# One attention block on one Trainium2 core: every engine's whole program and the list of loads as fixed lists

## The chip, the cores and the metric

The kernel runs on one core of a Trainium2 chip. The time is the device time of one execution in microseconds (us). The engines named here are TensorE (PE; its weight loads are shown as PEld), VectorE (DVE), ScalarE (ACT) and SyncE (SP, whose queue issues all loads and stores). GpSimd (POOL) only writes the identity matrix at the start. Each engine works off its own program in order, and the engines wait for one another through semaphores.

## What is computed

```python
B, Sq, D = 8, 112, 640
H, Sk, Dh = 32, 512, 192
q = (x @ wq).reshape(B, Sq, H, Dh)              # transposed to b h q d
scores = einsum("bhqd,bhkd->bhqk", q, k_cache) * Dh ** -0.5
p = softmax(scores, axis=-1)
o = einsum("bhqk,bhkd->bhqd", p, v_cache)       # transposed to b q (h d)
return o @ wo
```

All arrays are bfloat16. The caches have 8 x 32 x 512 x 192 elements each, wq is 640 x 6144 and wo 6144 x 640.

## The kernel before

**Steps.** The 32 heads are taken in two halves of 16. A unit t (0 to 15) is one batch element and one half of the heads. A step n (0 to 63) is a quarter of a unit, four heads, so unit t has the steps 4t to 4t+3. Two neighbouring units (two batch elements) share one product with wq and one with wo: m numbers these pairs (0 to 7) and lp the pairs of heads in them (0 to 7).

**Operations.** The program is a set of named operations, each with its engine, its dependencies and its instructions (class Plan, line 12). On TensorE they are:

- ("X", c) transposes a block of x (line 281), and ("K", t, u) a head of k for the first two units (line 295). From unit 2 on k arrives transposed, through a transposing load (line 149) on SP's queue.
- ("Qa", m, lp) and ("Qb", m, lp) are the two parts of q = x wq for two heads, 10 and 5 matmuls (line 329).
- ("S", n) is the scores of a step: 16 whole matmuls and then 16 on half of the rows each (lines 384 to 399). They always use the banks 0 to 3 of PSUM (of 8).
- ("PT", n, j) transposes the softmax of two heads (line 447), and ("PV", n) multiplies it with v (lines 475 and 486).
- ("O", u, f, part) is a piece of o wo (line 520), in 14 groups u of four pieces f, of 12 or 24 matmuls, cut in two parts. ("O6", ...), ("OL", ...) and ("OF", b) are the last group in other cuts and the final transposes of the output (lines 559, 583 and 608).

Each of these leaves its result in a bank, and the next user of the bank waits until it has been taken out. ScalarE takes out q (evQa, evQb, line 335), the values (evPV, line 496) and half of the transposed softmax (evPT with j = 0, line 453), and computes the exponentials with their sums (exp, line 417). VectorE takes out the scores with their minimum into one of two buffers (smax, line 412), divides (rc, norm, lines 429 and 421), takes out the other half of the transposed softmax (evPT with j = 1), adds up the output (oacc, lines 536 and 538), and makes the copies of q (qc, lines 361 and 362): two copies that put parts of q from partitions 0 to 63 into 64 to 127 and the other way round, since a head has 192 = 128 + 64 rows. Results of "X" and "K" go to either of the two. S(n+1) waits for the four smax of step n and for qc(n+1); smax(n, i) waits for the exp two before it; PV(n) waits for both evPT(n).

**The order.** Three stretches set it. The first nine steps follow lists written out by hand, FRONT_PE, FRONT_ACT and FRONT_DVE (lines 711 to 770), and the loads follow FRONT_SP. The steps 9 to 57 come from a loop (lines 783 to 824): each step puts on TensorE S(n), PV(n-2), Qa, the first part of an O, PT(n-1), the rest of the O and Qb, and on the other engines a fixed pattern. Which q and which O fall into which step is told by q_at and o_at (lines 619 to 628): one q to a step, except in steps 18 and 19, which have none (q_at leaves them out), and one O. The last six steps follow TAIL and two lists (lines 265 to 274 and 838 to 859). In the steps 57 to 61 a transposing transfer on SP's queue, ("TD", n), does the work of PT.

**SP's queue.** Loads are issued in one order. ("KN", t, lo, n) loads k for the transposes on TensorE, ("K", t, 0) is the transposing load of a unit, ("V", t, 0 or 8) half a unit's v, ("WQ", half, lp) a piece of wq, ("WO", half, u) one half of a half's wo. V waits for the PV that last used its buffer, K(t) for the last S of unit t-2, and the second half's WQ and WO for the last use of the first half's.

## Time and profile before

| what | us |
|---|---|
| median of 3 runs | 453.37 (451.6 to 454.62) |
| the profiled execution | 452.17 |
| its span, first to last instruction | 450.2 |
| TensorE busy in the span | 438.4 (97%) |
| VectorE busy | 367.8 (82%) |
| ScalarE busy | 338.4 (75%) |

The granted clock of TensorE was 0.999. The profiled execution is 1.2 us under the median, and 1.97 us of it lie outside its span. A row of the timeline has the start, the time, the engine, the line and operation, the tiles and how many instructions are merged in it; in brackets stands the idle time ahead of it and what ended it. The time of a matmul in such a row includes its way through the array, so that neighbouring rows overlap: what one costs is read from its start to the start of the next.

### The profile page before, as it was taken

Reading aid. Unit: us, or ns where it says so; the run is one execution under the profiler, and the core shown is the slowest. Engines: PE = TensorE matmul, PEld = TensorE weight load, DVE = VectorE, ACT = ScalarE, POOL = GpSimd, SP = SyncE. Lnnn points to the kernel's source line nnn. Section 1 sums busy time; section 2 is a strip of 40 time slices with the busy share of each in tenths; the row PEclk is TensorE's granted clock in tenths of the full one; section 3 lists DMA queues with packets and bytes.
Section 4 is the critical chain, followed back from the end, with each engine's and each line's share of the span. In section 5 each row is a group of like instructions: output and inputs, shape, how many; then the busy total and the mean of one; then the engine's idle time right before and its main releaser. Section 6 shows DMA issues by size and latency. Waiting matters only on the chain.

```text
span 450.2 us, 15025 instructions
## 1 busy us (share of the span) xinstructions
PE 438.4 (97%) x6345; PEld 402.8 (89%) x6345; DVE 367.8 (82%) x1172; ACT 338.4 (75%) x787; POOL 0.7 (0%) x6
## 2 busy tenths in 40 slices
...
GB/s 296 373 376 359 238 302 245 250 328 277 261 275 279 315 240 352 232 336 258 274 290 232 287 229 341 261 261 363 227 306 187 276 220 217 273 244 269 223 193 67
DMA packets 232547, 121.94 MB, mean 271 GB/s; under 512 B 182560, under 2 KB 232480, under 8 KB 232480
## 3 DMA queue, kind: packets, MB, share of 16 engines
...
HBM read 73.50 MB, written 1.15 MB: 166 GB/s over the span
## 4 chain that ended last, share of the span: by engine, by line
PE 85%; DMA 6%; DVE 4%; ACT 4%; issue 1%; SPq 0%; DVEq 0%; ACTq 0%
PE ps L329 18%; PE ps L520 17%; PE ps L486 11%; PE ps L447 10%; PE ps L397 7%; PE ps L475 6%; PE ps L384 6%; PE ps L386 6%; DMA wo_sb<-in_wo_dram 3%; DVE s_sb L412 3%; ACT p_sb L417 2%; PE ps L295 2%; DMA wq_sb<-p_sb 1%; DMA wq_sb<-in_wq_dram 1%; PE ps L583 1%
## 5 line engine op out<-in xcount | busy, mean ns | idle before, releaser
L417 ACT ACTIVATE p_sb<-s_sb,nmx 112x512 bf16<-112x512 f32 x256 | 183.2, 716 | 83.2 <-DVE s_sb L412 79.7
L412 DVE TENSOR_SCALAR_CACHE_REDUCE s_sb<-ps 112x512 f32<-112x512 f32 x256 | 167.5, 688 | 40.4 <-ACT p_sb L417 19.4
L329 PE MATMUL ps<-xT_sb,wq_sb 128*128 128x224 bf16 x960 | 111.1, 259 | 0.6 <-issue 0.4
L520 PE MATMUL ps<-oT_sb,wo_sb 128*128 128x224 bf16 x840 | 96.6, 259 | 1.8 <-DMA wo_sb<-in_wo_dram 1.8
L329 PEld LDWEIGHTS ps<-xT_sb,wq_sb 128*128 128x128 bf16 x960 | 88.6, 98 | 2.1 <-issue 0.9
L421 DVE TENSOR_SCALAR p_sb<-p_sb,rinv 112x512 bf16<-112x512 bf16 x256 | 79.3, 350 | 3.9
L520 PEld LDWEIGHTS ps<-oT_sb,wo_sb 128*128 128x128 bf16 x840 | 78.3, 98 | 2.1 <-DMA wo_sb<-in_wo_dram 2.1
L335 ACT ACTIVATE qr<-ps 128x448 bf16<-128x448 f32 (+1 forms) x112 | 49.1, 442 | 15.7 <-PE ps L329 15.6
L447 PE MATMUL ps<-ident,p_sb 112*128 112x112 bf16 x944 | 57.2, 213 | 1.2 <-ACT oT_sb L496 0.9
L453 ACT ACTIVATE pT_sb<-ps 128x896 bf16<-128x896 bf16 x59 | 53.5, 906 | 1.8 <-PE ps L447 1.1
L486 PE MATMUL ps<-pT_sb,vt 128*128 128x112 bf16 x912 | 54.8, 213 | 0.0
L447 PEld LDWEIGHTS ps<-ident,p_sb 112*128 112x128 bf16 x944 | 51.5, 98 | 3.4 <-ACT oT_sb L496 2.6
L486 PEld LDWEIGHTS ps<-pT_sb,vt 128*128 128x128 bf16 x912 | 45.8, 98 | 4.5
L417 ACT ACTIVATION_READ_ACCUMULATOR p_sb<-s_sb,nmx 112x1 f32 x256 | 49.0, 191 | 0.0
L496 ACT ACTIVATE oT_sb<-ps 128x672 bf16<-128x672 f32 x64 | 45.6, 712 | 3.8 <-PE ps L486 3.8
L453 DVE COPY pT_sb<-ps 128x896 bf16<-128x896 bf16 x59 | 36.4, 617 | 5.2 <-PE ps L447 5.2
L384 PE MATMUL ps<-kt,qh 128*112 128x256 bf16 x128 | 34.9, 273 | 0.0
L386 PE MATMUL ps<-kt,qh 128*112 128x256 bf16 x128 | 34.9, 272 | 0.0
L475 PEld LDWEIGHTS ps<-pT_sb,vt 128*64 128x64 bf16 x912 | 24.9, 109 | 10.9 <-issue 9.6
L475 PE MATMUL ps<-pT_sb,vt 128*64 128x112 bf16 x912 | 33.3, 216 | 0.8 <-issue 0.6
L399 PE MATMUL ps<-kt,qh 64*112 64x256 bf16 x128 | 34.0, 291 | 0.0
L384 PE MATMUL ps<-kt,qr 128*112 128x256 bf16 x112 | 30.7, 274 | 1.9 <-DVE qh L362 1.0
...
## 6 DMA issues: line engine op xcount, KB each, us to landing
vt<-in_v_cache_dram SPq DMA_DIRECT2D x31, 1536.0 KB, 8.4
...
wo_sb<-in_k_cache_dram SPq DMA_DIRECT2D x3, 1536.0 KB, 12.7
wo_sb<-in_k_cache_dram SPq DMA_DIRECT2D x2, 768.0 KB, 8.8
wq_sb<-in_v_cache_dram SPq DMA_DIRECT2D x1, 1536.0 KB, 8.0
...
```

Source lines behind the costliest of these rows:

```text
L329: mm = e.matmul(ps[:, bank, j * S2:(j + 1) * S2], wq_sb[:, dc, c0:c0 + 128], xT_sb[:, dc, bp * S2:(bp + 1) * S2], start=(dc == 0), stop=(d ...
L335: return e.activation(q_home(m, lp)[:, blocks[0]:blocks[0] + n, :], ps[:, bank, 0:n * S2].rearrange("p (c s) -> p c s", c=n), ACTF.Copy)
L384: e.matmul(ps[0:SQ, 2 * j, hs], ev, ktb[:, :, 0, cs(i)], start=(h == 0), stop=False, skip_group_check=True)
L386: mm = e.matmul(ps[0:SQ, 2 * j + 1, hs], od, ktb[:, :, 2, cs(i)], start=(h == 0), stop=False, skip_group_check=True)
L412: return e.tensor_scalar(s_sb[:, a, :].rearrange("p (e c) -> p e c", e=2), ps[0:SQ, 2 * j:2 * j + 2, h * 256:(h + 1) * 256], -scale, None, ...
L417: return e.activation(p_sb[:, k, :], s_sb[:, a, :], ACTF.Exp, bias=nmx[:, k:k + 1], scale=-1.0, accum_out=rsum[:, k:k + 1])
L421: return e.tensor_scalar(p_sb[:, k, :], p_sb[:, k, :], rinv[:, k:k + 1], None, op0=ALU.mult)
L447: mm = e.transpose(psb[:, bank, c:c + SQ], p_sb[:, (4 * n + 2 * j + h) % 8, q * 128:(q + 1) * 128], ident[0:SQ, 0:SQ])
L453: return e.activation(dst, src, ACTF.Copy) if j == 0 else e.tensor_copy(dst, src)
L475: mm = e.matmul(ps[64 * h:64 * h + 64, b0 + j, SQ:2 * SQ], vtb[:, h0 + 2 * j + h, d0:d0 + 64], pT(j, h, q), start=(q == 0), stop=(q == 3))
L486: mm = e.matmul(ps[:, b0 + j, 2 * h * SQ:(2 * h + 1) * SQ], vtb[:, h0 + 2 * j + h, d0:d0 + 128], pT(j, h, q), start=(q == 0), stop=(q == 3))
L520: mm = e.matmul(ps[:, o_bank(u, f), j * S2:(j + 1) * S2], wo_sb[:, KU * (u % 2) + k, m * 128:(m + 1) * 128], oT_sb[:, u % NO, k, :], start ...
```

## The change

The loop over the steps goes, and with it q_at, o_at and the three kinds of lists. In their place stand four lists for the whole kernel: ORDER_PE (548 operations), ORDER_ACT, ORDER_DVE and ORDER_SP. The same operations are in them, with two kinds of exceptions: eight copies of k (the heads 0, 1, 2, 8, 9 and 15 of unit 0, 0 and 5 of unit 1) go from ScalarE to VectorE and two (10 of unit 0, 2 of unit 1) the other way, and the copies of three blocks of x go from VectorE to ScalarE. An entry of ORDER_PE has its bank as its last number where it can choose, so that q also uses the banks 0 to 3 all through the kernel. Some dependencies are written out that the old order kept by itself (WQ, WO, oacc). The instructions of each operation and the way operations wait for one another stay as they are.

```diff
-            add("SP", ("WQ", half, lp), [("Qb", 3, lp + n - 1)] if half else [], emit, f"mWQ{lp}", 16)
+            add("SP", ("WQ", half, lp), [("Q" + q, 3, lp + i) for i in range(n) for q in "ab"] if half else [], emit, f"mWQ{lp}", 16)
...
-            old = [("O", 6 + u, 3, 1)] if half else [("KT", 1, HU - 1)]
+            first, last = u * KB // 2 * D // 768, ((u + 1) * KB // 2 * D - 1) // 768
+            old = [("O", 6 + u, 3, 1)] if half else [("KT", t, v) for t in range(2) for v in range(first, last + 1)]
...
+        ORDER_PE = [
+            ("X", 0, 0, "DVE"), ("X", 1, 6, "ACT"), ("Z", 10), ("Qb", 0, 1, 6), ("Qa", 0, 1, 4),
+            ("K", 0, 3, 5, "DVE"), ("Qa", 0, 0, 3), ("K", 0, 1, 7, "DVE"), ("K", 0, 2, 2, "DVE"),
+            ("K", 0, 0, 0, "DVE"), ("Qb", 0, 0, 7), ("Qb", 0, 3, 6), ("Qa", 0, 2, 4), ("S", 0), ("Qb", 0, 2, 7),
+            ("K", 0, 4, 6, "DVE"), ("Qa", 0, 3, 5), ("K", 0, 5, 6, "DVE"), ("K", 0, 7, 1, "ACT"),
+            ("K", 0, 6, 5, "DVE"), ("Qb", 0, 4, 0), ("Qa", 0, 4, 7), ("S", 1), ("K", 0, 8, 6, "DVE"),
...
+            ("O", 2, 0, 0, 7), ("PT", 15, 1), ("PT", 15, 0), ("O", 2, 0, 1, 7), ("S", 17), ("PV", 15),
+            ("O", 2, 1, 0, 7), ("Qa", 3, 1, 6), ("S", 18), ("PT", 16, 0), ("Qb", 3, 1, 6), ("PT", 16, 1),
+            ("O", 2, 1, 1, 7), ("PV", 16), ("O", 2, 2, 0, 7), ("PT", 17, 1), ("O", 2, 2, 1, 7), ("PT", 17, 0),
+            ("S", 19), ("PV", 17), ("O", 2, 3, 0, 7), ("O", 2, 3, 1, 7), ("Qb", 3, 3, 6), ("PT", 18, 0),
+            ("PT", 18, 1), ("S", 20), ("PV", 18), ("O", 3, 0, 0, 7), ("Qa", 3, 2, 1), ("Qa", 3, 3, 6),
...
+            ("O", 7, 2, 0, 7), ("O", 7, 2, 1, 7), ("PT", 37, 1), ("Qa", 5, 4, 1), ("Qb", 5, 7, 6), ("PT", 37, 0),
+            ("S", 39), ("PV", 37), ("O", 7, 3, 0, 7), ("Qa", 5, 5, 1), ("Qb", 5, 5, 0), ("PT", 38, 1),
+            ("O", 7, 3, 1, 7), ("PT", 38, 0), ("Qb", 5, 6, 6), ("S", 40), ("PV", 38), ("Qa", 5, 6, 7),
+            ("Qa", 5, 7, 1), ("O", 8, 0, 0, 7), ("O", 8, 0, 1, 7), ("PT", 39, 1), ("PT", 39, 0), ("S", 41),
+            ("PV", 39), ("O", 8, 1, 0, 7), ("O", 8, 1, 1, 7), ("PT", 40, 1), ("PT", 40, 0), ("S", 42), ("PV", 40),
+            ("O", 8, 2, 0, 7), ("Qa", 6, 0, 6), ("PT", 41, 0), ("O", 8, 2, 1, 7), ("PT", 41, 1), ("Qb", 6, 1, 6),
+            ("S", 43), ("PV", 41), ("O", 8, 3, 0, 7), ("Qb", 6, 3, 6), ("Qa", 6, 1, 1), ("Qb", 6, 0, 5),
...
+            ("O6", 1, 0, 7), ("O6", 1, 1, 7), ("S", 62), ("O6", 0, 0, 5), ("O6", 2, 0, 7), ("O6", 0, 1, 5),
+            ("OF", 5, 4), ("O6", 2, 1, 7), ("S", 63), ("PV", 60, 6), ("PV", 61), ("PT", 62, 1, 6), ("PT", 62, 0, 0),
+            ("OL", 0, 0), ("OF", 4, 1), ("OL", 1, 0), ("PT", 63, 0), ("PV", 62, 2), ("PT", 63, 1, 1), ("OL", 0, 1),
...
+        ORDER_ACT = [
+            ("evX", 1), ("evQa", 0, 0), ("evQb", 0, 1), ("evQa", 0, 1), ("evQb", 0, 0), ("evQb", 0, 3),
+            ("evQa", 0, 2), ("exp", 0, 0), ("evQb", 0, 2), ("evQa", 0, 3), ("exp", 0, 1), ("evK", 0, 7),
...
+        ORDER_DVE = [
+            ("evX", 0), ("evK", 0, 3), ("evK", 0, 1), ("evK", 0, 2), ("evK", 0, 0), ("qc", 0), ("smax", 0, 0),
+            ("smax", 0, 1), ("evK", 0, 4), ("smax", 0, 2), ("evK", 0, 5), ("qc", 1), ("evK", 0, 6), ("smax", 0, 3),
+            ("smax", 1, 0), ("smax", 1, 1), ("rc", 0, 1), ("evK", 0, 8), ("rc", 0, 0), ("smax", 1, 2), ("norm", 0, 2),
...
+            ("smax", 50, 1), ("norm", 49, 3), ("norm", 49, 1), ("smax", 50, 2), ("qc", 51), ("smax", 50, 3),
+            ("oacc", 10, 2), ("evPT", 49, 1), ("qc", 52), ("rc", 50, 0), ("rc", 50, 1), ("smax", 51, 0),
+            ("smax", 51, 1), ("norm", 50, 0), ("norm", 50, 1), ("smax", 51, 2), ("oacc", 10, 3), ("qc", 53),
+            ("norm", 50, 2), ("smax", 51, 3), ("norm", 50, 3), ("evPT", 50, 1), ("rc", 51, 0), ("norm", 51, 0),
...
+        ORDER_SP = [
             ("X", 0), ("WQ", 0, 0), ("KN", 0, 0, 4), ("WQ", 0, 2), ("KN", 0, 4, 4), ("WQ", 0, 4), ("KN", 0, 8, 8),
-            ("WQ", 0, 6), ("V", 0, 0), ("X", 1), ("KN", 1, 0, 8), ("V", 0, 8), ("KN", 1, 8, 8), ("V", 1, 0),
-            ("X", 2), ("K", 2, 0), ("V", 1, 8), ("WO", 0, 0), ("V", 2, 0), ("K", 3, 0), ("V", 2, 8), ("WO", 0, 1),
-            ("V", 3, 0), ("K", 4, 0), ("V", 3, 8), ("V", 4, 0), ("K", 5, 0), ("V", 4, 8), ("WQ", 1, 0), ("V", 5, 0),
-            ("K", 6, 0), ("V", 5, 8), ("WQ", 1, 2), ("V", 6, 0)]
-        assert sorted(order["SP"][:len(FRONT_SP)]) == sorted(FRONT_SP)
-        order["SP"][:len(FRONT_SP)] = FRONT_SP
-
-        del order["SP"][-3:]
-        order["SP"] += [
-            ("TD", 57), ("V", 14, 8), ("TD", 58), ("OUT", 0), ("TD", 59), ("V", 15, 0), ("TD", 60), ("OUT", 1),
-            ("TD", 61), ("OUT", 3), ("V", 15, 8), ("OUT", 4), ("OUT", 5), ("OUT", 2), ("OUT", 6), ("OUT", 7)]
-
-
-        END = NN - 6
-        NF = 9
-
-        TAIL = [
...
-        end_bank = {tok[:-1]: tok[-1] for tok in TAIL if tok[0] not in ("S", "OL")}
-
+            ("WQ", 0, 6), ("X", 1), ("V", 0, 0), ("KN", 1, 0, 8), ("X", 2), ("V", 0, 8), ("KN", 1, 8, 8), ("V", 1, 0),
+            ("K", 2, 0), ("V", 1, 8), ("WO", 0, 0), ("V", 2, 0), ("K", 3, 0), ("V", 2, 8), ("WO", 0, 1), ("V", 3, 0),
+            ("K", 4, 0), ("V", 3, 8), ("V", 4, 0), ("K", 5, 0), ("V", 4, 8), ("WQ", 1, 0), ("V", 5, 0), ("K", 6, 0),
+            ("V", 5, 8), ("V", 6, 0), ("K", 7, 0), ("V", 6, 8), ("WQ", 1, 2), ("WQ", 1, 4), ("V", 7, 0), ("K", 8, 0),
+            ("V", 7, 8), ("WQ", 1, 6), ("V", 8, 0), ("K", 9, 0), ("V", 8, 8), ("V", 9, 0), ("K", 10, 0), ("V", 9, 8),
+            ("WO", 1, 0), ("V", 10, 0), ("K", 11, 0), ("V", 10, 8), ("WO", 1, 1), ("V", 11, 0), ("K", 12, 0),
+            ("V", 11, 8), ("V", 12, 0), ("K", 13, 0), ("V", 12, 8), ("V", 13, 0), ("K", 14, 0), ("V", 13, 8),
+            ("V", 14, 0), ("K", 15, 0), ("TD", 57), ("V", 14, 8), ("TD", 58), ("TD", 59), ("V", 15, 0), ("TD", 60),
+            ("OUT", 1), ("OUT", 0), ("TD", 61), ("V", 15, 8), ("OUT", 2), ("OUT", 5), ("OUT", 4), ("OUT", 3),
+            ("OUT", 6), ("OUT", 7)]
+        bank_of = {}
+        for kind, *a in ORDER_PE:
+            size = {"PV": 1, "PT": 2, "O": 3, "O6": 2, "OF": 1}.get(kind)
+            if size and len(a) > size:
+                bank_of[(kind, *a[:size])] = a[size]
...
-            deps = [("O", u, f, 1)] + ([("XT", B * SQ // 128 - 1)] if u == 0 else [])
+            deps = [("O", u, f, 1)] + ([("oacc", u - 1, f)] if u % 2 else []) + ([("XT", B * SQ // 128 - 1)] if u == 0 else [])
...
-        q_at = {n: [(1, n)] for n in range(4, 8)}
-        for m in range(2, NM):
-            for lp in range(LP):
-                q_at[8 * m - (8 if (m, lp) < (3, 2) else 6) + lp] = [(m, lp)]
-        o_at = {9: [(0, 0)], 10: [(0, 1)], 11: [(0, 2), (0, 3)], 13: [(1, 0)], 14: [(1, 1)], 15: [(1, 2), (1, 3)]}
-        for u in range(2, 2 * NM - 2):
-            for f in range(4):
-                if 4 * u + 8 + f < END:
-                    o_at[4 * u + 8 + f] = [(u, f)]
-        whole = [o for n, os_ in o_at.items() for o in os_ if n not in q_at]
+        whole = [(2, 2), (2, 3)]
...
-        FRONT_PE = [
...
-        for kind, *a in FRONT_PE:
+        for kind, *a in ORDER_PE:
...
-        act += FRONT_ACT
-        dve += FRONT_DVE
-        for n in range(NF, END):
...
-            act += [("exp", n, 0), ("exp", n, 1)] + [("evPV", n - 2)]
-            act += [("exp", n, 2)] + a_q + [("exp", n, 3)]
-            act += [("evPT", n - 1, 0)] + b_q
-
-            dve += [("rc", n, 0), ("norm", n, 0), ("norm", n, 1)]
-            dve += [("oacc", *os_[0])] if two else []
-            dve += [("qc", n + 1)] if not late and not early else []
-            dve += [("evPT", n - 1, 1)]
-            dve += [("oacc", *o) for o in (os_[1:2] if two else os_[:1])]
-            dve += [("rc", n, 1), ("norm", n, 2), ("norm", n, 3)]
-            dve += [("qc", n + 1)] if late else []
-
...
+        act += ORDER_ACT
+        dve += ORDER_DVE
+        order["SP"] = ORDER_SP
```

341 lines of the change are left out of this document (229 added, 112 removed), and 100 rows, old and new, of tables (FRONT_PE, ORDER_PE, TAIL).

## Prediction

> **What bounds the kernel now.** I read the page's chain of waits first, which is TensorE for the most part, then the table of waits of TensorE's weight loads (they come ahead of each matmul, so that their idle time is where TensorE's program stands still), then the timeline of one step of the loop.
>
> ```profile
> PEld ps L397 <- issue: 11.4, 64, 0.2
> PEld ps L475 <- issue: 10.3, 54, 0.8
> PEld ps L447 <- ACT oT_sb L496: 2.6, 6, 0.8
> PEld ps L520 <- DMA wo_sb<-in_wo_dram: 2.1, 1, 2.1
> PEld ps L384 <- DVE s_sb L412: 1.4, 2, 1.1
> PEld ps L384 <- DVE qh L362: 1.4, 2, 1.2
> PEld ps L475 <- ACT pT_sb L453: 1.0, 4, 0.5
> PEld ps L295 <- DVE s_sb L412: 0.7, 1, 0.7
> ```
>
> The columns are the sum, the count and the longest. The first two rows are no waits for anyone: 0.18 us stands ahead of each of the 64 groups of L397 and of 54 groups of L475, where full matmuls give way to halves of the array. An order can't take these out while S and PV stay what they are. The other rows are single events, and they are what a better order can win.
>
> ```profile
> 175.00:200.00 25.00, 25.00 (x365) 23.26 (x361) 21.67 (x69) 19.13 (x47) 0.00 (x0) 1.00 1.16 293
> ```
>
> ```profile
> 172.77 1.12 PE L329 MATMUL ps<-xT_sb,wq_sb 128*128 128x224 bf16 x10
> 173.73 0.93 PE L520 MATMUL ps<-oT_sb,wo_sb 128*128 128x224 bf16 x8
> 174.50 0.95 PE L447 MATMUL ps<-ident,p_sb 112*128 112x112 bf16 x16
> 175.28 0.55 PE L520 MATMUL ps<-oT_sb,wo_sb 128*128 128x224 bf16 x4
> 175.67 0.64 PE L329 MATMUL ps<-xT_sb,wq_sb 128*128 128x224 bf16 x5
> 176.15 0.27 PE L384 MATMUL ps<-kt,qr 128*112 128x256 bf16 x1
> ...
> 177.69 0.58 PE L475 MATMUL ps<-pT_sb,vt 128*64 128x112 bf16 x16
> ...
> 179.00 1.12 PE L329 MATMUL ps<-xT_sb,wq_sb 128*128 128x224 bf16 x10
> ```
>
> The first fence is a row of the table by stretches (PE, PEld, DVE, ACT, POOL): in the middle of the loop TensorE is busy all 25.00 us, VectorE 21.67, ScalarE 19.13. The second is one step, and the starts give the price of each operation on TensorE: Qa 0.96, eight matmuls of an O 0.77, the two PT 0.78, four of an O 0.39, Qb 0.48, S 1.54, PV 1.31, in all 6.23. Nothing can be gained inside such a step. The gain is bounded by the single waits: 1.4 + 1.4 + 2.6 + 2.1 + 1.0 + 0.7 = 9.2 us in the rows shown.
>
> **The change, part by part.** The work on TensorE is the same 548 operations. Where a PV doesn't follow an S, the step into half columns comes on top of the one out of half rows (0.18 us by its row, not more): eight PV stand so in the old order and nine in the new one, +0.1 us.
>
> *The wait for wo* (2.1 us). O(9, 0) waits for WO(1, 1).
>
> ```profile
> 277.54 0.37 SPq L164 DMA_DIRECT2D vt<-in_v_cache_dram  x1
> 277.95 20.65 SPq L149 DMA_TRANSPOSE kt<-in_k_cache_dram  x1
> ```
>
> ```profile
> 299.28 13.27 DMA wo_sb<-in_wo_dram
> ```
>
> On SP's queue V(10, 0) goes out when PV(37) ends, then K(11) holds the queue for 20.65 us, then come V(10, 8) and WO(1, 1), which lands at 299.28 + 13.27 = 312.55, or 35.0 us behind the start of that V. ORDER_SP has the four in the same order with the same releaser, so 35.0 stays. What changes is how much TensorE has to do in between. By the prices above, the old order has 33.2 us of work from the end of PV(37) to O(9, 0); the new one draws S(45), 1.54, and a q, 0.96 + 2 x 0.48, ahead of it, moves one PV and one transpose behind it, and comes out at 36.5 (all operations of the two lists between these points, added up). So the wait goes, with 1.5 us to spare, -2.1. The same sum for WO(1, 0) gives 33.2 and 34.7, which did not wait before and won't now.
>
> *WQ(1, 2) on SP's queue* moves behind V(6, 0), K(7) and V(6, 8). It goes out where WQ(1, 4) went, about 20 us after PV(21), and its first user Qa(4, 2) comes 33.2 us of work after PV(21). I cost it at nothing; its cover is those 13 us for a load of half the bytes of the WO above, which took 13.27 behind other traffic. Without that cover it would wait a microsecond or two, once.
>
> *The steps without q* (2.6 us).
>
> ```profile
> 147.20 1.31 PE L520 MATMUL ps<-oT_sb,wo_sb 128*128 128x224 bf16 x12
> 149.09 0.96 PE L447 MATMUL ps<-ident,p_sb 112*128 112x112 bf16 x16 [0.58 <-ACT oT_sb L496]
> ```
>
> In steps 18 and 19 only an O stands between PV and PT, 1.15 us, and PT waits for ScalarE to take PV out of its bank. The new order lays Qb(3, 1), Qa(3, 1), Qb(3, 3) and others there: from the end of S(18) to S(19) it has 5.8 us of work instead of 3.2. I take 2.1 of the 2.6 as gone.
>
> *The first three steps* (1.4 us of waits for qh).
>
> ```profile
> wo_sb<-in_k_cache_dram SPq DMA_DIRECT2D x1, 768.0 KB, 7.0
> ```
>
> ```profile
> wo_sb<-in_k_cache_dram SPq DMA_DIRECT2D x1, 1536.0 KB, 16.0
> ```
>
> ```profile
> 1.77 0.52 SPq L186 DMA_DIRECT2D wo_sb<-in_k_cache_dram  x1
> ...
> 5.55 2.56 SPq L186 DMA_DIRECT2D wo_sb<-in_k_cache_dram  x1
> ...
> 6.70 2.57 PE L329 MATMUL ps<-xT_sb,wq_sb 128*128 128x224 bf16 x25 [0.17 <-DMA wq_sb<-in_wq_dram]
> ```
>
> The first pieces of k land at 1.77 + 7.0 = 8.77 and (heads 8 to 15) 5.55 + 16.0 = 21.6, and the first eight loads are as before. q starts at 6.70. The new order asks for the first k after Qb and Qa, at 8.14: a new wait of 0.6. From there to K(0, 8) it has eight K at 0.33 (six transposes of 128 columns at the rate of the 16 of 112 columns in two PT: 0.78 / 16 x 6 x 128 / 112 = 0.33), four Qa, four Qb and two S, 11.5 us, so it asks for head 8 at 20.3, about 20.6 with some wait in S(1): a new wait of 1.0. Against this, qc(1) stands ahead of the last smax in ORDER_DVE and S(1)'s wait falls from 1.2 to some 0.35. Together +0.75. The start thus stays as long as its loads; step 2 begins where it did, near 28.4.
>
> *The steps 3 to 8.* The waits there are the rows L295 (0.7), half a dozen of 0.2 to 0.3, and shares of the rows for L447 and L384: 2.4 us. K(1, 14) no longer uses a bank of the scores, and three copies of x leave VectorE; but eight copies of k come to it, and the stretch is its fullest. Between 0 and 2.4 I take 1.5, since the longest single one has lost its cause.
>
> *VectorE around the copies of q.*
>
> ```profile
> 175.59 0.33 DVE L362 COPY qh<-qr 64x672 bf16<-64x672 bf16 x1
> 175.84 0.61 DVE L453 COPY pT_sb<-ps 128x896 bf16<-128x896 bf16 x1
> ```
>
> ```profile
> 70.51 0.33 DVE L362 COPY qh<-accT 64x672 bf16<-64x672 bf16 x1
> 70.87 0.35 DVE L421 TENSOR_SCALAR p_sb<-p_sb,rinv 112x512 bf16<-112x512 bf16 x1
> ```
>
> A copy out of PSUM follows the second copy of q after 0.25 us, while that still runs; a norm, which reads SBUF, follows only after 0.36. In the old lists 7 of the 64 qc are followed by a norm, rc, oacc or another qc, in the new ones 32: 25 x 0.11 = 2.8 us more of VectorE's time, and as much at most for what stands ahead. Spread over 64 steps that is 0.04 a step, and VectorE has 6.23 x 3.33 / 25 = 0.8 free in each; at nothing. If that cover were gone, it would be 2.8. [...]
>
> *Tighter places.* The old loop has an O's rest, Qb and S between PT(n) and PV(n), 2.4 us; in the new order it is S alone, 1.54, in 31 of the 48 steps 9 to 56 (3 before). And between a PV and the next user of its bank 1.15 us or less lie in about a dozen steps (2 before).
>
> ```profile
> 103.35 0.96 PE L447 MATMUL ps<-ident,p_sb 112*128 112x112 bf16 x16
> 104.33 0.72 ACT L417 ACTIVATE p_sb<-s_sb,nmx 112x512 bf16<-112x512 f32 x1
> 105.04 0.91 ACT L453 ACTIVATE pT_sb<-ps 128x896 bf16<-128x896 bf16 x1
> 105.99 0.58 PE L475 MATMUL ps<-pT_sb,vt 128*64 128x112 bf16 x16 [0.23 <-ACT pT_sb L453]
> ```
>
> This is one of the three. PT and S end at 103.35 + 0.78 + 1.54 = 105.67. The copy would have fitted (0.91 in 1.54), but an exp was ahead of it on ScalarE, and PV started 0.3 late; the other two, in steps 19 and 20, show no such wait. So 0.1 a place on average, 31 places: between 0 and 3.1. I take 1.2, nearer to 0, because the new list of ScalarE sets most of these copies behind exps whose scores are a step old.
>
> *The end.*
>
> ```profile
> 421.76 6.75 DMA wq_sb<-p_sb
> ```
>
> S(63) waits 1.1 us (row L384 <- L412) for exps that wait for this transposing transfer, TD(60). The new lists keep smax(61, 0) ahead of the last norm(60) as the old ones do, so it stays, and the last adds and stores follow in the same order. Nothing.
>
> The sum: -2.1 - 2.1 + 0.75 - 1.5 + 0.1 + 1.2 = -3.65. The profiled execution has 452.17, which makes 448.5; it lies 1.2 under the median of 453.37, so as a median of runs the forecast is **449.7 us**.
>
> **The rivals.**
>
> *A, slower: ScalarE's turn.* TensorE waits in every tight place for a copy behind an exp. If each of the 31 costs the 0.3 measured above, that is 9.3 instead of 1.2: 449.7 + 8.1 = 457.8. It decides from 0.15 a place (4.85 + 0.1 used up, no gain). For it: the steps are irregular, so that an exp meets a copy at another point in each. Against it: two of the three places did not wait, and ScalarE is idle for a quarter of the stretch shown (19.13 of 25).
>
> *B, the start is the loads' anyway and the steps 3 to 8 give nothing.* Then only wo and the steps without q are won: 449.7 + 1.5 = 451.2, or 452 with twice my price for the tight places. For it: VectorE takes six more copies of k there, and three fewer of x.
>
> *C, all waits close.* No tight place costs (-1.2), the steps 3 to 8 give all (-0.9), the 0.5 kept in the steps without q goes, and so does S(63)'s 1.1: 446.0.
>
> *D, the lists do not do what they say*: other waits of the same size take the place of the old ones, 453.4.
>
> **The chances.** 1% of 453.37 is 4.5 us, and that is about what a measurement of this kernel can tell from no change: faster means under 448.8, slower over 457.9. The forecast gets 0.50 (its own range 447.0 to 452.0, two fifths of it under 448.8), C 0.15, B 0.10, D 0.05, A 0.20, of which 0.12 lie beyond the mark because a place can cost more than the row. Faster 0.20 + 0.15 = 0.35, slower 0.12, the same 0.53. The range from 445.5 to 456.0 leaves out half of A and a little below C.
>
> **What would show it.** The row L520 <- DMA for wo should be gone, with O(9, 0) behind S(45). L447 <- ACT L496 should fall under 0.6. Two waits for loads of k should stand before 22 us, and S(63)'s wait should remain. The windows from 80 to 400 us should show TensorE at 25.00 or nearly. I am wrong if the rows L475 <- ACT L453 or L447 <- ACT L496 grow to several us (A), or if S waits for qh or s_sb in many steps, which would mean that VectorE's 2.8 us were on the path after all.

## The result and the profile after

| | before | after |
|---|---|---|
| median of runs (us) | 452.34 (449.68 to 454.62, 6 runs) | 445.71 (445.38 to 446.67, 6 runs) |
| the profiled execution, its span | 452.17, 450.2 | 445.84, 444.0 |

The ratio is 0.9858, with a 95% interval from 0.9822 to 0.9894: 6.4 us faster (4.8 to 8.1), where 3.65 were forecast. The profile before is the one shown above.

First the page of the changed kernel (busy time, share of the span, instructions), then the table of waits of TensorE's weight loads (sum, count, longest).

```profile
PE 436.8 (98%) x6345; PEld 402.5 (91%) x6345; DVE 361.2 (81%) x1175; ACT 343.0 (77%) x784; POOL 0.7 (0%) x6
```

```profile
PEld ps L704 <- issue: 11.4, 64, 0.2
PEld ps L782 <- issue: 6.6, 37, 0.2
PEld ps L602 <- DMA wo_sb<-in_k_cache_dram: 2.1, 2, 1.4
PEld ps L782 <- ACT p_sb L724: 1.8, 10, 0.2
PEld ps L782 <- ACT pT_sb L760: 1.4, 8, 0.2
...
PEld ps L754 <- issue: 0.9, 5, 0.2
PEld ps L636 <- DMA wq_sb<-in_wq_dram: 0.8, 1, 0.8
```

The lines have moved by the length of the lists: L704 is the half-row part of S that was L397, L782 the PV that was L475, L754 is PT (L447), L827 O (L520), L636 q (L329), L602 the transposes of k (L295). The 0.18 us ahead of the half arrays is all there: 11.4 at S, and at PV in rows of several names, none over 0.2 for one. Of the single waits of before, wo (2.1), PT on ScalarE's copies of PV (2.6), S on qh and on s_sb (1.4 and 1.4) and the load into a bank of the scores (0.7) are gone. New is L602, the two waits for the first loads of k. VectorE is not busier but less busy, 361.2 for 367.8. "Issue" in such a row is time in which the profile shows nothing that the engine waits for.

The table by stretches (PE, PEld, DVE, ACT, POOL, then the granted clock) shows the middle:

```profile
100.00:125.00 25.00, 25.00 (x347) 23.34 (x345) 20.62 (x69) 18.89 (x44) 0.00 (x0) 1.00 1.16 285
...
325.00:350.00 25.00, 25.00 (x367) 23.15 (x367) 20.85 (x69) 19.87 (x46) 0.00 (x0) 1.00 1.19 273
375.00:400.00 25.00, 24.89 (x343) 22.94 (x342) 21.01 (x70) 20.56 (x50) 0.00 (x0) 1.00 1.18 266
```

TensorE is busy throughout, but for one place behind 375 us, to which the experiments come back.

A second reading gives the loss by stretch. For every operation of TensorE I took its start less the start of the one before, less the price of that one (S 1.54, PV 1.31, Qa 0.96 and so on, as in the prediction, and 0.10 where a PV does not follow an S). The prices come to 430.4 before and 430.5 after; what is left over is the time that TensorE lost:

| stretch | lost before | lost after | change | forecast |
|---|---|---|---|---|
| to S(3), the first three steps | 2.76 | 2.84 | +0.08 | +0.75 |
| S(3) to S(9) | 2.67 | 0.44 | -2.23 | -1.5 |
| S(9) to S(44), with steps 18 and 19 | 2.40 | 1.13 | -1.27 | -2.1 |
| S(44) to S(46), wo | 2.00 | 0.06 | -1.94 | -2.1 |
| S(46) to S(58) | 0.61 | 0.58 | -0.03 | 0 |
| S(58) to the end | 1.56 | 0.53 | -1.03 | 0 |
| tight places, in steps 9 to 56 | | in the rows above | | +1.2 |

The sum of the changes is -6.4, the prices add 0.1, and the spans differ by 6.3 (450.24 and 443.97). The last row after holds another 0.1 that is a price and no wait: ten PV have no S ahead of them in the new order, for eight in the old one, and the tenth, PV(61), stands behind PV(60), which takes 1.41 there.

### The profile page after: what moved, and what is told of

Its sections match the earlier page's. It is cut to its first block, busy times and chain, and to the rows that moved or that the text cites. A ratio compares the mean times of both kernels' runs of the same rounds, so it can differ in the third digit from the quotient of the medians.

```text
span 444.0 us, 15055 instructions
## 1 busy us (share of the span) xinstructions
PE 436.8 (98%) x6345; PEld 402.5 (91%) x6345; DVE 361.2 (81%) x1175; ACT 343.0 (77%) x784; POOL 0.7 (0%) x6
## 3 DMA queue, kind: packets, MB, share of 16 engines
HBM read 73.50 MB, written 1.15 MB: 168 GB/s over the span
## 4 chain that ended last, share of the span: by engine, by line
PE 94%; DMA 4%; SPq 1%; DVE 0%; ACT 0%; issue 0%
PE ps L636 19%; PE ps L827 18%; PE ps L793 13%; PE ps L754 11%; PE ps L704 8%; PE ps L782 7%; PE ps L691 6%; PE ps L693 6%; DMA wo_sb<-in_k_cache_dram 4%; PE ps L602 2%; PE ps L866 1%; PE ps L890 1%; SPq L198 1%; PE ps L915 0%; PE ps L588 0%; SPq L186 0%
## 5 line engine op out<-in xcount | busy, mean ns | idle before, releaser
L719 DVE TENSOR_SCALAR_CACHE_REDUCE s_sb<-ps 112x512 f32<-112x512 f32 x256 | 172.1, 684 | 32.9 <-PE ps L706 16.5
L636 PE MATMUL ps<-xT_sb,wq_sb 128*128 128x224 bf16 x960 | 106.1, 259 | 0.6 <-DMA wq_sb<-in_wq_dram 0.6
L827 PE MATMUL ps<-oT_sb,wo_sb 128*128 128x224 bf16 x840 | 93.9, 259 | 0.0
L636 PEld LDWEIGHTS ps<-xT_sb,wq_sb 128*128 128x128 bf16 x960 | 89.4, 98 | 1.7 <-DMA wq_sb<-in_wq_dram 0.8
L728 DVE TENSOR_SCALAR p_sb<-p_sb,rinv 112x512 bf16<-112x512 bf16 x256 | 82.0, 347 | 1.7
L827 PEld LDWEIGHTS ps<-oT_sb,wo_sb 128*128 128x128 bf16 x840 | 77.9, 98 | 0.3 <-issue 0.2
L754 PE MATMUL ps<-ident,p_sb 112*128 112x112 bf16 x944 | 60.5, 213 | 0.0
L642 ACT ACTIVATE qr<-ps 128x224 bf16<-128x224 f32 (+1 forms) x112 | 47.6, 445 | 14.7 <-PE ps L636 14.3
L754 PEld LDWEIGHTS ps<-ident,p_sb 112*128 112x128 bf16 x944 | 53.2, 97 | 2.2 <-issue 0.9
L706 PE MATMUL ps<-kt,qh 64*112 64x256 bf16 x128 | 34.0, 291 | 0.0
L782 PEld LDWEIGHTS ps<-pT_sb,vt 128*64 128x64 bf16 x912 | 24.8, 109 | 10.1 <-issue 5.9
L782 PE MATMUL ps<-pT_sb,vt 128*64 128x112 bf16 x912 | 33.3, 216 | 0.0
L704 PE MATMUL ps<-kt,qh 64*112 64x256 bf16 x128 | 31.2, 269 | 0.0
```

The source lines that it names most:

```text
L636: mm = e.matmul(ps[:, bank, j * S2:(j + 1) * S2], wq_sb[:, dc, c0:c0 + 128], xT_sb[:, dc, bp * S2:(bp + 1) * S2], start=(dc == 0), stop=(d ...
L704: m1 = e.matmul(ps[0:SQ, 2 * j, hs], ev, ktb[0:64, :, 1, cs(i)], start=False, stop=True, skip_group_check=True)
L719: return e.tensor_scalar(s_sb[:, a, :].rearrange("p (e c) -> p e c", e=2), ps[0:SQ, 2 * j:2 * j + 2, h * 256:(h + 1) * 256], -scale, None, ...
L728: return e.tensor_scalar(p_sb[:, k, :], p_sb[:, k, :], rinv[:, k:k + 1], None, op0=ALU.mult)
L754: mm = e.transpose(psb[:, bank, c:c + SQ], p_sb[:, (4 * n + 2 * j + h) % 8, q * 128:(q + 1) * 128], ident[0:SQ, 0:SQ])
L782: mm = e.matmul(ps[64 * h:64 * h + 64, b0 + j, SQ:2 * SQ], vtb[:, h0 + 2 * j + h, d0:d0 + 64], pT(j, h, q), start=(q == 0), stop=(q == 3))
```

## The experiments

All kernels are written as fixed lists in the changed kernel's code, so that their lines are its lines or a few more. "Old" in a label is the order of the kernel before. Each comes with a ratio to the kernel before on the same chip, whose median was 451.76 beside new_front, new_front_middle, old_wo_late and new_front_fill, 452.43 beside old_lists, new_old_loads and the two with qc_cut, and 453.10 beside the other four.

### Front alone; front and middle

Two joined lists: the changed order as far as a certain S, and from there the old one.

```diff
 ("Qa", 2, 0, 6), ("PT", 7, 0), ("PT", 7, 1), ("S", 9), ("PV", 7),
-("Qa", 2, 1, 6), ("O", 0, 0, 0, 7), ("PT", 8, 0), ("O", 0, 0, 1, 7), ("PT", 8, 1), ("S", 10),
+("Qa", 2, 1, 6), ("O", 0, 0, 0, 7), ("PT", 8, 0), ("PT", 8, 1), ("O", 0, 0, 1, 7), ("Qb", 2, 1, 6), ("S", 10),
...
```

> The changed kernel's lists up to the scores of step 9, with its first loads, and from there the order of the kernel before. Theory 1 (the gain is the sum of single waits of TensorE, each with its own cause): by the starts of the matmuls, what TensorE lost up to S(9) was 4.9 us before and is 3.0 in the changed kernel, so this kernel takes 1.9 us less than the kernel before, some 450.4 against 452.3, and keeps the wait for wo of 2.1, the two waits of PT in steps 18 and 19 (2.6 together in L447 <- ACT) and the wait of 1.1 at S(63). Theory 2 (the gain is VectorE's order around the copies of q, a little in each of the 64 steps): 6.3 us over 64 steps are 0.1 a step, nine steps give 0.9, 451.4. Theory 3 (the new list of loads gives it): all of its early part is in here, so more than 1.9 comes.

Measured: 449.32, ratio 0.9960 (0.9936 to 0.9984), so 1.8 less than before: theory 1's number. Theory 3 asked for more, and theory 2's 0.9 lies within the interval too. The waits of the middle are there:

```profile
PEld ps L828 <- DMA wo_sb<-in_wo_dram: 2.3, 1, 2.3
PEld ps L603 <- DMA wo_sb<-in_k_cache_dram: 2.1, 2, 1.4
PEld ps L755 <- ACT oT_sb L804: 1.9, 4, 0.8
PEld ps L755 <- DVE s_sb L720: 1.2, 1, 1.2
```

The last row is the seam's own (the first old step with a bank of the scores still in use). One wait that I expected is missing: S(63) doesn't wait, with the old last six steps in place. So theory 1's number is met in part by luck: in this profile the front loses 2.2 less than before, the seam 1.2 more, S(63) 1.1 less and wo 1.9 more. The runs are spread besides: 4 of the 12 had a mean granted clock of 0.995 or 0.996 and took 452.2 on average, the other eight, at 0.999 or 1.000, took 448.9. The wait for wo, below, is the likely reason.

```diff
 ("S", 57), ("PV", 55), ("O", 12, 1, 0, 7), ("O", 12, 1, 1, 7),
-("S", 58), ("PT", 56, 0), ("OF", 2, 6), ("PT", 56, 1), ("Qb", 7, 6, 7), ("Qb", 7, 7, 0), ("Qa", 7, 7, 1),
+("Qa", 7, 7, 6), ("Qb", 7, 6, 7), ("PT", 56, 0), ("PT", 56, 1), ("Qb", 7, 7, 6), ("S", 58), ("OF", 3, 4),
...
```

> The changed kernel's lists up to the scores of step 58, and behind them the last six steps as they were before; with new_front it cuts the change into front, middle and tail. Theory 1: the middle lost 4.65 us before and loses some 0.9 now, so this kernel takes 3.75 us less than new_front, 5.7 less than the kernel before (446.6 against 452.3), and about 1.0 more than the changed kernel, with the wait of 1.1 at S(63) still there. The share of the middle is two single events, wo and the steps 18 and 19, so the stretches from 100 to 400 us show TensorE at 25.00 but for them in both kernels. Theory 2: the middle's 49 steps give 4.8 and the tail 0.6. If the tail's gain is not its own order's but comes from when the loads of the middle land, S(63) does not wait here and the time is that of the changed kernel, 445.7.

Measured: 447.75, ratio 0.9914 (0.9884 to 0.9943), 3.9 less than before and not 5.7, with runs from 446.4 to 451.3. The profiled execution took 446.41, its span 444.6, and it shows neither wo nor PT on PV, so the middle's single waits are gone as theory 1 has it. S(63) does not wait here either, so the tail's wait did not come back with the old tail. The last row here stood at 0.2 in the changed kernel:

```profile
PEld ps L603 <- DMA wo_sb<-in_k_cache_dram: 1.9, 2, 1.2
...
PEld ps L828 <- issue: 1.1, 1, 1.1
```

That is O(12, 1) behind PV(55), in the stretch that was not full above. What the slower executions of this kernel lost can't be read, since only one was profiled.

### The wait for wo

```diff
-("PV", 42), ("Qa", 6, 2, 6), ("O", 9, 0, 0, 7), ("PT", 43, 0), ("PT", 43, 1), ("O", 9, 0, 1, 7), ("Qb", 6, 2, 6), ("S", 45),
+("PV", 42), ("Qa", 6, 2, 6), ("PT", 43, 0), ("PT", 43, 1), ("Qb", 6, 2, 6), ("S", 45), ("O", 9, 0, 0, 7), ("O", 9, 0, 1, 7),
```

> The order of the kernel before, with both parts of O(9, 0) behind S(45) and its addition to the output behind smax(45, 1). Theory 1: the row of wo <- DMA (2.1) goes, one more PV stands without an S ahead of it, and the time falls by about 2.0, to 450.3 against 452.3 (ratio 0.9956). Rival (the wait only hides another, for a copy or for the scores): the row goes, another wait of the same size stands within the next two steps, and the time stays within 0.5 of the kernel before.

Measured: 449.90, ratio 0.9957 (0.9940 to 0.9974), 1.9 less, as theory 1 has it. The row for wo is gone. By the trace the matter is less tidy: with O(9, 0) away, PT(43) waits for ScalarE's copy of PV(42), which O(9, 0) had covered,

```profile
311.59 0.96 PE L755 MATMUL ps<-ident,p_sb 112*128 112x112 bf16 x16 [0.50 <-ACT oT_sb L804]
```

0.67 from start to start, and Qb another 0.34. So half of the 1.97 came back beside it (the rival's case in part), and S(63)'s 1.06 was missing again. That the time still fell by 1.9 raised the question what the wait costs in other executions of the old order. That is the next kernel, with nothing changed but that its order is written as lists.

> The order of the kernel before, every list of it, written as fixed lists in the changed kernel's code: nothing differs from the kernel before but line numbers. Theory 1 (the waits of the kernel before belong to its order): the same rows as before, wo 2.1, PT on ScalarE's copies of PV 2.6, qh 1.4, the load of half-banks 0.7, and S(63) on the last scores 1.1; span 450.2. Rival (part of what went in the changed kernel is one execution's chance): new_front and old_wo_late have the old last six steps without the wait at S(63), because the transposing transfer TD(60) took 5.5 and 5.7 us there and 6.8 in the kernel before; then this execution has no such wait either, nor the 0.5 on issue at O(11, 1), and a span near 448.6, with all the other rows as before.

Measured in a single run: 454.68, span 452.7. All rows of before are there, wo with 3.9 in place of 2.1, S(63) with 0.24 in place of 1.06, and nothing on issue at O(11, 1). So the rival is right that the two last belong to an execution, but wrong on the span, because of wo. Rows of the table by stretches, two microseconds each, for before,

```profile
310.00:312.00 2.00, 0.78 (x9) 0.53 (x6) 1.90 (x7) 2.00 (x6) 0.00 (x0) 1.00 1.07 372
312.00:314.00 2.00, 1.41 (x21) 1.41 (x22) 0.77 (x3) 1.11 (x4) 0.00 (x0) 1.00 1.05 371
314.00:316.00 2.00, 2.00 (x26) 1.82 (x23) 1.57 (x5) 1.24 (x2) 0.00 (x0) 1.00 1.58 193
```

for this one,

```profile
312.00:314.00 2.00, 0.00 (x0) 0.00 (x0) 1.06 (x4) 1.37 (x5) 0.00 (x0) 1.00 1.07 369
314.00:316.00 2.00, 1.14 (x12) 1.11 (x13) 0.00 (x0) 0.00 (x0) 0.00 (x0) 0.89 1.07 375
316.00:318.00 2.00, 2.00 (x21) 1.84 (x19) 0.56 (x1) 0.92 (x1) 0.00 (x0) 0.50 1.64 254
318.00:320.00 2.00, 2.00 (x16) 1.66 (x16) 1.14 (x5) 0.36 (x1) 0.00 (x0) 0.76 0.87 194
```

and for new_front, which has the old middle:

```profile
310.00:312.00 2.00, 0.20 (x2) 0.20 (x3) 1.72 (x7) 2.00 (x6) 0.00 (x0) 1.00 1.06 373
312.00:314.00 2.00, 2.00 (x25) 2.00 (x24) 0.00 (x0) 0.68 (x2) 0.00 (x0) 0.70 1.06 369
314.00:316.00 2.00, 2.00 (x13) 1.68 (x12) 1.70 (x5) 0.49 (x2) 0.00 (x0) 0.50 1.31 155
```

The column to read is the granted clock, third from the right. Behind the wait it fell to 0.50 in the last two kernels and stayed at 1.00 in the first. There the operations between the wait and S(45) cost nearly twice their price, 1.5 to 1.7 more. So this wait cost 2.0 in the execution that I had, 2.2 + 1.65 in new_front and 3.84 + 1.53 in old_lists. To see whether a longer wait brings the clock down again, one kernel comes earlier to it:

```diff
-("S", 44), ("PV", 42), ("Qa", 6, 2, 6), ("O", 9, 0, 0, 7), ("PT", 43, 0),
+("S", 44), ("PV", 42), ("O", 9, 0, 0, 7), ("Qa", 6, 2, 6), ("PT", 43, 0),
```

> The order of the kernel before with the first part of O(9, 0) ahead of Qa(6, 2) and not behind it, so that TensorE comes 0.96 earlier to the wait for wo. In the profile of before TensorE stood still for 2.0 there at a granted clock of 1.00 throughout; in new_front 2.2 and in old_lists 3.8, and there the clock fell to 0.50 for some 3 us behind the wait, which cost another 1.5. Theory (the price of this wait in the old order is the wait and a slower clock behind it, and the forecast's 2.1 was its smallest case): a wait of 3 to 5, the clock at half behind it, and a time 1 to 2.5 above the kernel before. Rival (the 1.5 have another cause): no clock under 0.9 there, and the time is that of the kernel before, since Qa(6, 2) then fills behind the wait what it filled ahead of it.

Measured: 454.45, ratio 1.0022 (0.9999 to 1.0045), 1.0 more than before. TensorE waited 3.3, and the clock fell:

```profile
PEld ps L828 <- DMA wo_sb<-in_wo_dram: 3.3, 1, 3.3
```

```profile
310.00:312.00 2.00, 0.00 (x0) 0.00 (x0) 1.94 (x7) 1.89 (x5) 0.00 (x0) 1.00 1.06 370
312.00:314.00 2.00, 1.10 (x9) 1.01 (x10) 0.72 (x3) 0.00 (x0) 0.00 (x0) 0.86 1.06 376
314.00:316.00 2.00, 2.00 (x14) 1.65 (x13) 0.00 (x0) 0.01 (x1) 0.00 (x0) 0.50 1.67 256
```

The wait and the slow clock are the theory's. The loss against the runs of before is at its lower edge, and many of those have the lower clock too. The record has each run's mean granted clock, which was 0.999 in the profile of before and 0.995 in that of old_lists. At 0.996 or less were 3 of 17, 5 of 11 and 12 of 17 runs of before on the three chips (by 1.1 to 2.5 us slower, on average, than the others beside them) and 8 of 10 of old_wo_early, but none of the six of old_wo_late, and 2 of the 39 of the kernels with the new front and middle and uncut copies of q (one of the two lost its time elsewhere, below; the other was not profiled). So the old order meets the slower clock in a share of its executions, and without this wait it is rare.

### Is it VectorE's time around the copies of q?

Each of the two copies of a step is cut into six; data and result stay.

```diff
-                e.tensor_copy(qh[64:128, n % 2, :, 0:3, :], src[0:64])
-                return e.tensor_copy(qh[0:64, n % 2, :, 1:4, :], src[64:128])
+                for j in range(2):
+                    for c in range(3):
+                        e.tensor_copy(qh[64:128, n % 2, j, c, :], src[0:64, j, c, :])
+                for j in range(2):
+                    for c in range(3):
+                        last = e.tensor_copy(qh[0:64, n % 2, j, 1 + c, :], src[64:128, j, c, :])
+                return last
```

> The changed kernel with each of the two copies of q of a step cut into six of a sixth (same data, same result): twelve VectorE instructions in place of two, some 1.0 to 1.9 us a step where two took 0.66 (12 times 0.08, the shortest VectorE instruction of the page, to 12 times 0.16, the reciprocal's), so 0.3 to 1.3 more in a step of 6.8 in which VectorE is idle for 1.3. Theory 1 (VectorE has time to spare in the new order as in the old one, and the gain was single waits): up to half a microsecond a step costs next to nothing, within 2 us of the changed kernel; both orders lose the same. Theory 2 (the new order is made around VectorE's time at these copies, and lives by it): it loses more than the old order does.

> The order of the kernel before with the same twelve copies in place of two. Beside new_qc_cut: theory 1, the same loss as in the new order; theory 2, a smaller one in the old order; and a third case, a larger loss in the old order, would mean that the new one bears more VectorE time, so that its gain is in part VectorE's.

Measured: 470.10 in the new order (ratio 1.0389, 1.0355 to 1.0423) and 476.77 in the old one (1.0539, 1.0503 to 1.0575). Against its own uncut order each lost 24.4 us (470.10 - 445.71 and 476.77 - 452.43; by the ratios, 1.0389 / 0.9858 = 1.0539 and 1.0539). The copies of q in the new order, now

```profile
L673 DVE COPY qh<-qr 64x112 bf16<-64x112 bf16 x336 | 38.8, 188 | 0.8
L670 DVE COPY qh<-qr 64x112 bf16<-64x112 bf16 x336 | 37.8, 179 | 2.7 <-ACT qr L642 1.0
```

take 87.5 with the 96 that read accT, for 42.1 uncut, 0.71 more in each step. So both orders give back a little over half of it (24.4 of 45.4). The places differ. In the new order, with the rows of PT on the norms, S on qh and S on the scores:

```profile
PEld ps L759 <- DVE p_sb L733: 8.1, 15, 1.2
PEld ps L696 <- DVE qh L673: 5.7, 10, 1.3
PEld ps L696 <- DVE s_sb L724: 3.7, 12, 0.6
```

and in the old one, nearly all at one:

```profile
PEld ps L697 <- DVE qh L674: 22.2, 34, 1.9
```

Theory 1 has the equal loss right and "next to nothing" wrong, as more was added than the half microsecond that it spoke of. Theory 2 falls: the new lists do not live by VectorE's time at these copies, nor do they bear more of it. They spread such a delay over three kinds of waits, where the old order has one.

### The list of loads

The new order with the loads in the old order (two loads of x, WQ(1, 2) and the stores at the end).

```diff
-("WQ", 0, 6), ("X", 1), ("V", 0, 0), ("KN", 1, 0, 8), ("X", 2), ("V", 0, 8), ("KN", 1, 8, 8), ("V", 1, 0), ("K", 2, 0),
+("WQ", 0, 6), ("V", 0, 0), ("X", 1), ("KN", 1, 0, 8), ("V", 0, 8), ("KN", 1, 8, 8), ("V", 1, 0), ("X", 2), ("K", 2, 0),
...
-("V", 5, 8), ("V", 6, 0), ("K", 7, 0), ("V", 6, 8), ("WQ", 1, 2), ("WQ", 1, 4), ("V", 7, 0),
+("V", 5, 8), ("WQ", 1, 2), ("V", 6, 0), ("K", 7, 0), ("V", 6, 8), ("WQ", 1, 4), ("V", 7, 0),
...
```

> The changed kernel's order on every engine with the list of loads of the kernel before. Theory (the loads' new order gives nothing by itself): no load that a TensorE wait ends on moves, so 445.7, within 0.5. Rival (WQ(1, 2) behind K(7), x earlier, or the first store later, is part of the gain): a wait for x or for wq appears that the changed kernel does not have, 1 to 2 us, 447 or more.

Measured: 447.97, ratio 0.9895 (0.9857 to 0.9933), with runs from 445.54 to 450.26. The interval takes in the changed kernel's 0.9858, and no wait for x or for wq is there that the changed kernel does not have. Its profiled execution (span 446.4) lost 1.1 and 1.2 us in rows put on issue, at PV(42) and at O(12, 1), and 0.5 at PV(62). The first is in truth a late load of v: V(10, 8) landed at 306.00 and PV(42) started at 306.14, while both copies that it needs had ended at 304.46. The last is one too, V(15, 8). At V(10, 8) the two lists have the same loads in the same order. By its median this kernel is nearer to the rival's "447 or more", by the rows the rival's waits are not there. Whether the list of loads is worth a microsecond or two stays open.

### The first loads of k

```diff
-("Qa", 0, 1, 4), ("K", 0, 3, 5, "DVE"), ("Qa", 0, 0, 3), ("K", 0, 1, 7, "DVE"),
+("Qa", 0, 1, 4), ("Qa", 0, 0, 3), ("K", 0, 3, 5, "DVE"), ("K", 0, 1, 7, "DVE"),
...
-("S", 1), ("K", 0, 8, 6, "DVE"), ("K", 0, 13, 7, "DVE"), ("K", 0, 11, 5, "DVE"), ("Qa", 0, 5, 4),
+("S", 1), ("Qa", 0, 5, 4), ("K", 0, 8, 6, "DVE"), ("K", 0, 13, 7, "DVE"), ("K", 0, 11, 5, "DVE"),
```

> The changed kernel with two operations moved: Qa(0, 0) ahead of K(0, 3) and Qa(0, 5) ahead of K(0, 8). Theory: the two transposes wait 0.64 and 1.23 us for their loads, and the work put ahead of them (0.96 each) fills the waits, so 0.6 to 1.0 of the one and 0.96 of the other go: 1.0 to 1.6 less than the changed kernel, 444.1 to 444.7. Rival (the first steps are set by the loads and by VectorE's copies of k behind them, not by TensorE): the waits for loads go, S(0), S(1) or S(2) start no earlier, and the time stays at 445.7.

Measured: 445.11, ratio 0.9847 (0.9826 to 0.9867), beside 0.9858 for the changed kernel. The waits for k fell from 2.1 to 0.3, but q, moved forward, came too early for its own loads:

```profile
PEld ps L636 <- DMA wq_sb<-in_wq_dram: 1.4, 4, 0.5
...
PEld ps L602 <- DMA wo_sb<-in_k_cache_dram: 0.3, 1, 0.3
```

S(9) started at 75.51 in place of 76.16: 0.65 won (0.42 against the second profile of the changed kernel, below), where 1.0 to 1.6 were expected. Even that is hardly more than scatter: in four other kernels with the changed kernel's order up to there, S(9) starts between 75.60 and 76.03. The other way is to cut the load:

```diff
-("KN", 0, 4, 4), ("WQ", 0, 4), ("KN", 0, 8, 8), ("WQ", 0, 6),
+("KN", 0, 4, 4), ("WQ", 0, 4), ("KN", 0, 8, 4), ("KN", 0, 12, 4), ("WQ", 0, 6),
```

> The changed kernel with the load of the heads 8 to 15 of the first unit cut into two halves, in the same place of the list. Theory: K(0, 8) waits 1.23 for a load of 1536 KB that lands at 21.6, of which it needs the first head; by the bytes, 2.5 us before the whole the half is there, and the wait goes: 1.2 less than the changed kernel, 444.5, and none of the new waits for wq that came when other work was put in front (1.4 in new_front_fill). Rival (the front is as long as its loads, whatever their cut): K(0, 8) starts earlier and K(0, 12) or a Qb waits instead, S(3) starts at 35.4 as before, 445.7.

> The changed kernel once more, for a second profiled execution of it. Theory (what is left of its scatter is TensorE's wait for its own program): the piece of 16 KB on the instruction queue that TensorE needs behind PV(55) came at 388.52 here, and at 389.01, 389.94 and 390.38 in the three other kernels with this order, and O(12, 1) waited 0.27, 1.15, 2.28 and 1.18; O(12, 1) waits again, between 0 and 2.5, and no other wait differs by more than 0.3 from the first execution. Rival (the first execution was a lucky one and the waits of the kernel before come back): waits of 1 us or more stand at S or PV for qh, s_sb or pT_sb. Time 445.7 and up to 2 more.

Measured on the same chip: 446.28 with the cut, ratio 0.9842 (0.9812 to 0.9871), and 446.19 for the changed kernel once more, 0.9846 (0.9813 to 0.9879). No difference. The wait at K(0, 8) went as the theory has it, and S(3) started at 34.72, 0.4 before the 35.12 of the changed kernel beside it (34.81 to 35.36 in all kernels with that front). Then the time was lost elsewhere:

```profile
PEld ps L603 <- DMA wo_sb<-in_k_cache_dram: 1.0, 2, 0.8
PEld ps L828 <- DMA wo_sb<-in_wo_dram: 1.0, 1, 1.0
```

O(9, 0) came earlier and waited for wo again, whose second half landed at 311.56, as it did at 311.53 in the changed kernel beside it. So no version beat the changed kernel by more than its scatter.

### TensorE's wait for its own program

The changed kernel's second profile (span 447.7, time 449.46, while the five other runs took 445.18 to 446.27) lost 3.6 us at one place, at PV(55); by the starts, its other waits are those of the first profile within 0.4. In new_front_fill 2.3 were lost there. Rows of the timeline, for the one and the other:

```profile
389.97 0.58 PE L782 MATMUL ps<-pT_sb,vt 128*64 128x112 bf16 x16
390.49 0.91 PE L793 MATMUL ps<-pT_sb,vt 128*128 128x112 bf16 x15
393.17 0.24 PE L793 MATMUL ps<-pT_sb,vt 128*128 128x112 bf16 x1 [1.77 <-issue]
```

```profile
389.46 0.91 PE L793 MATMUL ps<-pT_sb,vt 128*128 128x112 bf16 x15
392.49 0.21 PE L793 MATMUL ps<-pT_sb,vt 128*128 128x112 bf16 x1 [2.11 <-issue]
```

The break lies within PV(55), ahead of its last matmul, where no operation has a wait: at the same instruction each time. In new_again the granted clock fell behind it (0.80, 0.50 and 0.84 in the three stretches of 2 us from 392), which makes 3.6 of 1.9; in new_front_fill it stayed at 1.00. The page of the changed kernel has a queue for instructions (packets, MB, share):

```profile
q8 instruction: 50, 0.82, 0.7%
```

That is 16 KB a packet, and 65 bytes for each of the 12,690 matmuls and weight loads of TensorE, so I take it for TensorE's program, some 250 instructions a piece. Two stops of new_old_loads bear this out: counted with the instructions that only wait, TensorE has 12,833 in 50 pieces, 257 a piece, and ahead of the stop in PV(55) there is one of 0.5 in PV(51), 768 instructions or three pieces earlier. The trace has each packet's time. For the piece with number 42, counted from 0, in the kernels with the new order:

| kernel | piece lands | last matmul of PV(55) starts | behind it | lost |
|---|---|---|---|---|
| changed kernel | 389.50 | 391.12 | 1.62 | 0.27 |
| new_front_middle | 390.10 | 391.59 | 1.49 | 1.15 |
| new_old_loads | 391.46 | 393.05 | 1.59 | 1.18 |
| new_again | 391.66 | 393.17 | 1.51 | 1.93 |
| new_front_fill | 391.08 | 392.49 | 1.41 | 2.28 |
| new_kn_split | 389.84 | 391.29 | 1.45 | 0.03 |
| new_plain_k | 387.31 | 390.28 | 2.97 | 0.00 |

The matmul starts 1.4 to 1.6 behind the landing wherever it was late, whatever the landing time. K(15), a transposing load, was in flight then (378.43 to 399.95 in the changed kernel). The last row is the test of that, a kernel that leaves out the transposition:

```diff
-                return e.dma_start_transpose(dst, src)
+                return e.dma_start(kt[t % 2][:].rearrange("p a m c -> p (a m c)")[:, lo * 768:hi * 768]
+                    .rearrange("p (u x) -> p u x", u=hi - lo), k_cache[b, half * HU + lo:half * HU + hi]
+                    .rearrange("u (r q) d -> r u (q d)", q=4))
```

> The changed kernel with the 14 transposing loads of k as plain loads of the same bytes into the same place, so that from unit 2 on the scores are those of a k that is not transposed: the output is not the reference's. Theory (a transposing load in flight holds up the pieces of TensorE's program, and that is the wait on issue): all pieces come when TensorE is 190 to 310 instructions past the start of the piece two before, none at 330 or more as in the 13 cases of a transposing load in flight; O(12, 1) does not wait, and the time is some 0.3 to 1 below the changed kernel with less scatter. Rival (the pieces come late for another reason, the load of v or TensorE's own pace): one still comes at 350 or more and a wait on issue of a microsecond stands somewhere behind 200 us.

Measured: 444.98, ratio 0.9816 (0.9785 to 0.9846), with all runs between 444.94 and 445.49, where the changed kernel on the same chip had 445.18 to 449.46. The window of two microseconds that holds the place is full, at 2.00, and so are its neighbours:

```profile
388.00:390.00 2.00, 2.00 (x39) 1.56 (x38) 1.91 (x7) 1.87 (x5) 0.00 (x0) 1.00 1.05 372
390.00:392.00 2.00, 2.00 (x28) 2.00 (x26) 2.00 (x9) 2.00 (x6) 0.00 (x0) 1.00 1.00 347
```

By the expectation's count, how far TensorE is past the start of the piece two before when a piece sets out, 330 or more are reached by five pieces in the changed kernel while a transposing load was in flight and by one later, and here by two (331 and 347), so not by none. Before and after have ten under a transposing load between them, not the "13" of the expectation. The theory holds in the main: without transposing loads the piece lands 2.2 to 4.4 us earlier than in the six kernels above and nothing waits. A load of k was in flight here too (K(15), 377.86 to 393.67), so it isn't any load of k that delays the piece. Why a transposing one does, the trace doesn't say, and there is one profile without them.

## Why the forecast had the sign and not the size

The profiled executions took 445.84 where the sum gave 448.5. As medians the distance is larger, 445.71 for 449.7, mostly because the 1.2 added for the median of before came from three runs; with six it was 452.34, 0.2 above its profiled execution. The time lies below the forecast's own range (447.0 to 452.0), at C.

**The wait for wo** (-2.1): right that O(9, 0) behind S(45) ends it, and it measured -1.94 between the two profiles. But the step took one execution's size for the size. In the two other profiles of this stretch in the old order, new_front and old_lists, it cost 3.8 and 5.4 with the slower clock, which the trace of before, with 1.00 all through, did not show. And "so 35.0 stays" failed: from V(10, 0) to the landing of wo it was 35.0 to 35.4 in six profiles of either order (before, new_front, new_front_middle, new_front_fill, old_wo_late, old_wo_early) and 36.5 to 37.6 in five (changed kernel, new_again, new_kn_split, new_old_loads, old_lists); new_plain_k and the two with qc_cut are left aside. Where it was short in the new order, the forecast 1.5 were to spare (1.4 and 1.6). Where it was long, they weren't: in the changed kernel wo landed at 311.11 and O(9, 0) started at 311.19, and in new_again and new_kn_split it waited 0.3 and 1.0. That the wait was gone altogether in the profile of the changed kernel is in part luck.

**Steps without q** (-2.1 of 2.6): the row L447 <- ACT L496 is gone altogether. From S(9) to S(44), where these steps lie, TensorE lost 1.27 less. The row's 2.6 held some 0.1 in each of its six places that isn't lost from start to start (by starts the five in this stretch make 1.8), and the new order has some 0.8 of small losses there, none over 0.12, that the old one has not.

**The first three steps** (+0.75): the two new waits came as forecast, at K(0, 3) 0.64 for 0.6 and at K(0, 8) 1.23 for 1.0. S(1)'s wait, put at 0.35, went completely, and so did one of 0.35 at K(0, 3) for a copy of k (the row L295 <- ACT L301), which the step left out; the stretch came out at +0.08.

**Steps 3 to 8** (-1.5 of 2.4): -2.23; nearly all went. With the row above, the front gives -2.15 by the trace, for a forecast of -0.75; new_front's 1.8 by time holds the seam and S(63) too.

**Tight places** (+1.2): this step failed. In the steps 9 to 57, 45 PV follow an S; all of them together lost 0.31 us, the worst 0.05. One place of three with a 0.3 was made into a rate for 31, although the step itself named why it should be less: the new list of ScalarE sets the copies behind exps whose scores are a step old. Rival A falls with it.

**VectorE** (0): right. The later starts are there: in 29 of the 32 places in the new lists (12 norm, 8 rc, 6 oacc, 3 qc) the next instruction starts 0.36 behind the second copy of q, as here,

```profile
171.69 0.33 DVE L669 COPY qh<-qr 64x672 bf16<-64x672 bf16 x1
172.05 0.35 DVE L728 TENSOR_SCALAR p_sb<-p_sb,rinv 112x512 bf16<-112x512 bf16 x1
```

but VectorE's busy time did not grow (361.2 for 367.8), no S waits for qh or s_sb any more, and an addition of 0.71 a step costs both orders the same, 24.4. So the trace shows the later start, 0.36, where smax and the copies out of PSUM follow after 0.25 at the earliest, and no run here shows a price for it on the path.

**The end** (0): wrong for the pair of profiles, -1.03, and the reason was that the step kept S(63)'s wait for TD(60) as part of the order. TD(60) took 5.9 to 7.1 in the three profiles of the old last steps where S(63) waited, and 5.5 to 5.7 in the three where it didn't; in the six with the new last steps it took 4.1 to 4.9 and S(63) never waited. In the old list TD(60) is issued some 5.7 behind V(15, 0), in the new one some 7.6. That this distance is the cause fits these twelve profiles, but was not tried by itself (the two with qc_cut, where S(63) waits 0.1 and 0.4 with VectorE later throughout, are left aside). Since the wait was 1.06, 0.24, 1.37 and three times nothing under the old last steps, 0.4 on average, more than half of the -1.03 belongs to the profile of before, so to chance.

**The copies into half arrays** (+0.1): ten PV stand without an S ahead in the new order, not nine, so this was 0.1 short.

So rival C (446.0), all waits close, is nearest to what happened: no tight place costs, the steps 3 to 8 give nearly all, and S(63)'s wait goes. That its number is met so closely is luck: the 0.5 that C adds in the steps without q did not come; these steps gave less than forecast. The first three steps, which C left as they were, made up for half of that, and the median of before, put 1.0 too high, for most of the rest.
